# A second layer's seven products a unit: runs of four and three in place of pairs

## The chip, the cores and the metric

One Trainium2 chip, one of its cores. The metric is the device time of one execution in microseconds (us). TensorE does the matmuls and writes PSUM (eight banks), ScalarE and VectorE copy from PSUM and do the elementwise work, SyncE issues DMAs.

## The reference

Attention of a small state over `x` (8 batches, 8 heads, 512 positions and 32 state rows, width 64), and then two layers on its 4352 rows of 512 values:

```python
x = _attn_ref(x, state)                      # 8 x 544 rows of 512
h = np.maximum(x @ moe_w_in, 0.0)            # 512 -> 2048
x = (s * (h * h) + b) @ moe_w_out            # 2048 -> 512
h = np.maximum(x @ moe2_w_in, 0.0)           # the second layer
return (h * h) @ moe2_w_out
```

All in float32. The kernel splits each float32 operand into a high and a low part and adds three matmuls (high-high, high-low, low-high).

## The kernel before

The first 679 us hold the attention and the first layer; the change leaves them as they are. The second layer (`second_layer`, L716) goes through the rows in six parts: five of six tiles of 128 rows, and a last one of four. A part goes through eight units. A unit makes 256 columns of the hidden layer and multiplies them by the output weights.

The hidden columns of a unit are a 2 x 2 block product (two halves of the width 512, two halves of the part's rows, two blocks of 128 columns) with seven products in place of eight. The order is `PRODUCTS = (1, 6, 2, 5, 7, 3, 4)` (L54); this text calls them m0 to m6 by their place. Each product (L635) is six matmuls with 384 moving columns (256 in the last part). They lie in two PSUM banks of their own, pools `psa` and `psb`, taken in turns by the step's number. m0, m1, m3 and m4 begin a bank anew; m2, m5 and m6 add to what the bank still holds from m0, m3 and m4. So after each product, `drain` (L725) issues the instruction that reads the bank: ScalarE copies or rectifies m0, m2 and m3 (L654), VectorE adds m1 (`u2`, which also needs the copy of m0), m4 (`u3`, which also needs `u2`), m5 and m6 (L728). The next product on that bank waits for it. Behind the drains come the square and the split of the hidden values into `g` (L664, L668), partly one or two steps later.

The second product of a unit, hidden times output weights, is `mm2_second` (L672): for each of two blocks of 128 hidden columns and each tile of rows three matmuls with 512 moving columns (`o`, L686), 36 in a unit of six tiles, 24 in one of four. They add up in a bank per tile over the eight units of a part; behind the last ones the banks are copied out (L705, L707). `mm2_second(i - 1)` is issued during unit i, in shares: at each odd step, counted over all units, so much of it as corresponds to the place m. As a unit has seven steps, pairs of products and shares of about ten output matmuls alternate, and pairs lie across the border of two units. In unit 0 the share comes from the first layer's last 24 matmuls, of 256 columns.

Engines work in the order of issue. Behind each step's share, `jobs` issues what else is due there: in units 0 to 7 the sums and splits of the second input weights (L547, L555, L559) and the halves of the second output weights, 128 x 1024 each (L213 on ScalarE, L215 on VectorE), and in units 3, 4, 7 and 8 of the parts the inputs of the next part (`x_bias` L598, sums L607, `x_hi` L617 on ScalarE, `x_lo` L621 on VectorE). The last `x_lo`, for m6, is issued at m4 of the new part's first unit. From unit 8 on, `w_load` (L564) fetches a product's weights for two units later, behind the product.

Of the kernel before, what the change touches and what calls it, by code (L numbers as in the profile page):

```python
# [61 lines left out]
def attn_mlp2(ctx: ExitStack, tc: tile.TileContext, xT, xn, st, w_in1, w_out1, w_in2, w_out2, s_in, b_in, out):  # L62
# [34 lines left out]
    def pst(name, pool=None):  # L97
        return (pool or next(banks)).tile([P, 512], F32, tag="ps", name=name)
# [419 lines left out]
    def half(n):  # L518
        return len(parts[n]) // 2 * P
# [115 lines left out]
    def product(i, m, o, start):  # L635
        n, _ = units[i]
        w = w_at(i % 2, m).rearrange("p (h i c) -> p h i c", h=2, i=2)
        x = x_view(n, m)
        for k in range(2):
            for a, b in ((0, 0), (0, 1), (1, 0)):  # L640
                nc.tensor.matmul(  # L641
                    out=o, lhsT=w[:, a, k, :], rhs=x[:, b, k, :], start=(start and k + a + b == 0),
                    stop=(k + a == 2), skip_group_check=True,
                )
        w_load(i + 2, m)
# [26 lines left out]
    def mm2_second(i):  # L672

        n, u = units[i]
        nt = len(parts[n])
        if u == 0:
            for t in range(nt):
                pool, tag = (pa, "acc") if t < 4 else (psc, "ps")
                acc2[t] = pool.tile([P, 512], F32, tag=tag, name=f"o{n}{t}")
        for f in range(2):  # L680
            fa = 2 * u + f
            wh, wl = (w[:, fa % FQ, :] for w in W["o2", fa // FQ])
            for t in range(nt):
                g = g2[i, f][:, :, t * P : (t + 1) * P]
                for e, (l_, r_) in enumerate(((g[:, 0], wh), (g[:, 0], wl), (g[:, 1], wh))):
                    nc.tensor.matmul(  # L686
                        out=acc2[t], lhsT=l_, rhs=r_, start=(fa == 0 and e == 0), stop=(fa == NF - 1 and e == 2)
                    )
                    if fa == NF - 1 and e == 2:
                        out_tile(n, t)  # L690
                    yield
# [24 lines left out]
    def second_layer(between, rest):  # L716
# [84 lines left out]
        for i, (n, u) in enumerate(units):  # L801
            th = half(n)
            if i:
                flow.append((mm2_second(i - 1), 6 * len(parts[units[i - 1][0]])))
            for m, p in enumerate(PRODUCTS):
                step = i * len(PRODUCTS) + m
                pool = (psa, psb)[step % 2]
                if p in (1, 6, 5, 7):
                    c[p] = pst(f"m{p}", pool)[:, :th]
                out = c[{2: 1, 3: 5, 4: 7}.get(p, p)]  # L810
                product(i, m, out, p in (1, 6, 5, 7))
                drain(i, m, out)
                if step % 2:
                    while len(flow) > 1:
                        for _ in flow.pop(0)[0]:
                            pass
                        done = 0
                    upto = flow[0][1] * (m + 1) // len(PRODUCTS)
                    for _ in itertools.islice(flow[0][0], upto - done):
                        pass  # L820
                    done = upto
                for fn in jobs.pop((i, m), []):
                    fn()
# [208 lines left out]
    with tc.manual_schedule():  # L1032
# [50 lines left out]
        assert not side, sorted(side)  # L1083
        last = range(len(order) - LAG, len(order))
        second_layer(between, itertools.chain(*(mm2(*order[i], gs.pop(i)) for i in last)))


# [39 lines left out]
```

## Time and profile before

| | us |
|---|---|
| median of 3 runs | 1398.97 |
| lowest and highest | 1397.71, 1399.82 |
| the profiled execution | 1398.62 |
| its span, first to last instruction | 1396.8 |
| TensorE busy, share of the span | 1379.9, 99% |
| VectorE busy | 765.1, 55% |
| ScalarE busy | 759.2, 54% |

The mean granted clock of TensorE over the span is 0.991 of full speed. Matmuls are pipelined: one starts before the one ahead has ended, so a row's duration is longer than the distance to the next start, and a busy share of 99% does not mean that no time could be saved. Distances between starts are what the prediction works with.

### The profile page before, as it was taken

What the parts mean: (1) busy time and instruction counts of PE and PEld (TensorE: products, weight loads), DVE (VectorE), ACT (ScalarE), POOL (GpSimd) and SP (SyncE); (2) the same over time, 40 slices, a digit from 0 to 9 for tenths busy, and PEclk for the clock granted to TensorE, in tenths of its full rate; (3) what the DMA queues carried; (4) which work ended last, traced back from release to release, by engine and by line L of the source; (5) the groups of instructions that cost most, each with busy time, mean ns of one, the idle gap of its engine ahead of it and who ended that gap; (6) DMA issues with size and microseconds to landing.
All of it is one profiled execution on the core that took longest, in us unless ns stands there. A gap on an engine that the chain in (4) does not pass through costs nothing.

```text
span 1396.8 us, 20319 instructions
## 1 busy us (share of the span) xinstructions
PE 1379.9 (99%) x7822; PEld 1169.0 (84%) x7822; DVE 765.1 (55%) x1496; ACT 759.2 (54%) x1492; POOL 0.7 (0%) x7
## 2 busy tenths in 40 slices
PE   6999999999999999999999999999999999999998
PEld 4777777778777777889998999989999889998897
DVE  7888645555555867445677544453444435333433
ACT  5777656656666656557655543363344335433543
POOL 0000000000000000000000000000000000000000
PEclk7899999999999999999999999999999999999999
DMA  7365232332414241302673655445345533543652
GB/s 251 112 219 185 91 108 78 103 127 76 153 47 148 78 152 61 114 0 99 196 250 136 193 162 160 119 148 160 114 129 174 166 116 118 160 142 106 207 156 84
DMA packets 88432, 188.50 MB, mean 135 GB/s; under 512 B 8592, under 2 KB 25232, under 8 KB 85776
## 3 DMA queue, kind: packets, MB, share of 16 engines
q1 hardware_dynamic: 88192, 187.07, 42.2%
q8 instruction: 62, 1.02, 0.3%
q14 instruction: 34, 0.28, 0.1%
q10 hardware_dynamic: 144, 0.13, 0.0%
HBM read 144.18 MB, written 42.99 MB: 134 GB/s over the span
## 4 chain that ended last, share of the span: by engine, by line
PE 98%; DVE 1%; ACT 0%; issue 0%; POOLq 0%; POOL 0%
PE o L686 27%; PE acc L481 27%; PE m L641 24%; PE h L451 15%; PE S L263 2%; PE sr L416 1%; PE on L1030 1%; PE S L291 1%; PE sc L263 1%; PE tp L396 0%; DVE V L141 0%; DVE V L146 0%; PE S L306 0%; DVE m L365 0%; DVE t L366 0%; DVE t L379 0%
## 5 line engine op out<-in xcount | busy, mean ns | idle before, releaser
L481 PE MATMUL acc<-g,o1h 128*128 128x512 f32 (+1 forms) x1152 | 341.2, 379 | 0.0
L481 PEld LDWEIGHTS acc<-g,o1h 128*128 128x128 f32 x1152 | 211.4, 188 | 41.9 <-issue 2.2
L481 PE MATMUL acc<-g,o1l 128*128 128x512 f32 (+1 forms) x576 | 217.6, 378 | 0.4 <-DVE o1l L189 0.4
L451 PE MATMUL h<-aT,S 128*128 128x512 f32 x768 | 203.0, 400 | 3.0 <-ACT S L309 1.9
L451 PEld LDWEIGHTS h<-aT,S 128*128 128x128 f32 x768 | 142.6, 190 | 58.5 <-issue 10.9
L641 PE MATMUL m<-xw 128*128 128x384 f32 (+1 forms) x1008 | 183.1, 328 | 0.0
L641 PEld LDWEIGHTS m<-xw 128*128 128x128 f32 x1008 | 171.6, 188 | 7.5
L464 DVE TENSOR_TENSOR g<-r,g 128x512 fp32r<-128x512 f32 (+1 forms) x144 | 94.7, 658 | 112.0 <-ACT g L460 112.0
L654 ACT ACTIVATE sc<-sc 128x384 f32<-128x384 f32 (+1 forms) x144 | 72.8, 505 | 152.2 <-DVE sc L728 150.6
L458 ACT ACTIVATE r<-h 128x512 f32<-128x512 f32 (+1 forms) x144 | 82.1, 570 | 125.0 <-PE h L451 124.9
L654 ACT ACTIVATE v<-m 128x384 f32<-128x384 f32 (+1 forms) x96 | 45.5, 474 | 152.8 <-PE m L641 152.2
L481 PEld LDWEIGHTS acc<-g,o1l 128*128 128x128 f32 x576 | 108.4, 188 | 21.2 <-DVE o1l L189 0.9
L686 PE MATMUL o<-o2h,xw('g', 0)_6322 128*128 128x512 f32 x364 | 121.2, 392 | 0.0
L686 PE MATMUL o<-o2h,xw('g', 1)_6323 128*128 128x512 f32 x364 | 121.1, 392 | 0.0
L686 PE MATMUL o<-o2h,xw('g', 2)_6324 128*128 128x512 f32 x360 | 119.7, 392 | 0.0
L728 DVE TENSOR_TENSOR v<-m,r 128x384 f32<-128x384 f32 (+1 forms) x48 | 25.7, 535 | 167.3 <-PE m L641 167.3
L641 PE MATMUL m<-xw,xw('odd', 0)_6203 128*128 128x384 f32 (+1 forms) x576 | 107.3, 328 | 0.0
L641 PEld LDWEIGHTS m<-xw,xw('odd', 0)_6203 128*128 128x128 f32 x576 | 98.4, 188 | 3.8
L459 ACT ACTIVATE r<-r 128x512 f32<-128x512 f32 (+1 forms) x144 | 87.7, 609 | 4.6
L460 ACT ACTIVATE g<-r 128x512 fp32r<-128x512 f32 (+1 forms) x144 | 87.6, 609 | 4.6
L111 DVE TENSOR_TENSOR S<-S,S 128x512 fp32r<-128x512 f32 x54 | 34.8, 686 | 91.3 <-ACT S L110 91.3
L641 PE MATMUL m<-xw,xw('odd', 1)_6204 128*128 128x384 f32 (+1 forms) x432 | 79.3, 327 | 0.0
(150 smaller groups left out, 1909.4 us busy)
## 6 DMA issues: line engine op xcount, KB each, us to landing
xw<-w2s SPq DMA_DIRECT2D x140, 256.0 KB, 2.8
xw('odd', 0)_6203<-w2s SPq DMA_DIRECT2D x20, 1024.0 KB, 4.9
xw('odd', 1)_6204<-w2s SPq DMA_DIRECT2D x20, 768.0 KB, 4.3
i1r<-w_in SPq DMA_DIRECT2D x16, 512.0 KB, 5.2
xn<-xn SPq DMA_DIRECT2D x8, 1024.0 KB, 8.6
o1r<-w_out SPq DMA_DIRECT2D x16, 512.0 KB, 4.7
x<-ot SPq DMA_DIRECT2D x32, 256.0 KB, 2.9
i2r<-w_in SPq DMA_DIRECT2D x16, 512.0 KB, 5.2
```

The lines of the kernel that those rows point to most:

```text
L111: nc.vector.tensor_tensor(out=lo, in0=src, in1=hi.bitcast(F32), op=ALU.subtract)
L263: nc.tensor.matmul(out=outs[r][k * NS : (k + 1) * NS], lhsT=state[rows, r, k, :], rhs=moving(rows, k), start=True, stop=True, skip_group_c ...
L451: nc.tensor.matmul(out=hp, lhsT=l_, rhs=r_, start=(i == 0), stop=(i == len(ops) - 1))
L458: nc.scalar.activation(out=r, in_=hp, func=ACTF.Relu)
L459: nc.scalar.activation(out=r, in_=r, func=ACTF.Square)
L460: nc.scalar.activation(out=g[:, 0], in_=r, func=ACTF.Copy)
L464: nc.vector.tensor_tensor(out=g[:, 1], in0=r, in1=g[:, 0].bitcast(F32), op=ALU.subtract)
L481: nc.tensor.matmul(out=o, lhsT=l_, rhs=r_, start=(opens and i == 0), stop=(closes and i == 2))
L641: nc.tensor.matmul(out=o, lhsT=w[:, a, k, :], rhs=x[:, b, k, :], start=(start and k + a + b == 0), stop=(k + a == 2), skip_group_check=True,)
L654: nc.scalar.activation(out=c, in_=src, func=func)
L686: nc.tensor.matmul(out=acc2[t], lhsT=l_, rhs=r_, start=(fa == 0 and e == 0), stop=(fa == NF - 1 and e == 2))
L728: add = lambda o, x, y: nc.vector.tensor_tensor(out=o, in0=x, in1=y, op=ALU.add)
```

## The change

The share of output matmuls is issued behind m3 and behind m6 of each unit, in place of behind each odd step:

```diff
                 out = c[{2: 1, 3: 5, 4: 7}.get(p, p)]
                 product(i, m, out, p in (1, 6, 5, 7))
                 drain(i, m, out)
-                if step % 2:
+                if m in (3, 6):
                     while len(flow) > 1:
                         for _ in flow.pop(0)[0]:
                             pass
                         done = 0
                     upto = flow[0][1] * (m + 1) // len(PRODUCTS)
```

So m0 to m3 stand in one run, then 20 output matmuls (36 x 4 // 7; 13 with four tiles), then m4 to m6, then the other 16 (11). The banks go on in turns by the step's number: A, B, A, B, A, B, A in an even unit, the other way round in an odd one. Drains and jobs keep their steps.

## Rows read from the trace of the kernel before

**Rows 1.** The page's chain that ended last, by line.
```profile
PE o L686 27%; PE acc L481 27%; PE m L641 24%; PE h L451 15%; PE S L263 2%; PE sr L416 1%; PE on L1030 1%; PE S L291 1%; PE sc L263 1%; PE tp L396 0%; DVE V L141 0%; DVE V L146 0%; PE S L306 0%; DVE m L365 0%; DVE t L366 0%; DVE t L379 0%
```
**Rows 2.** Waits of TensorE: us in total, times, longest; last of seven.
```profile
PE acc L481 <- DVE o1l L189: 0.4, 1, 0.4
```
**Rows 3.** Timeline of TensorE, one pair: start, us, engine, line, tiles, count.
```profile
1009.28 1.23 PE L641 MATMUL m<-xw,xw('odd', 0)_6203 128*128 128x384 f32 x6
1010.35 1.20 PE L641 MATMUL m<-xw,xw('odd', 1)_6204 128*128 128x384 f32 x6
1011.39 0.39 PE L686 MATMUL o<-o2h,xw('g', 1)_6323 128*128 128x512 f32 x1
```
**Rows 4.** Timeline of TensorE, first layer, from one run of twelve to its end.
```profile
147.87 0.61 PE L481 MATMUL acc<-g,o1h 128*128 128x512 f32 x2
...
150.59 1.52 PE L451 MATMUL h<-aT,S 128*128 128x512 f32 x6
```
**Rows 5.** Timeline of TensorE, the first pair of units 22 and 24.
```profile
1018.33 2.27 PE L641 MATMUL m<-xw 128*128 128x384 f32 x12
...
1049.68 2.27 PE L641 MATMUL m<-xw 128*128 128x384 f32 x12
```
**Rows 6.** Timeline in the last part: products, output matmuls, two drains.
```profile
1327.09 1.60 PE L641 MATMUL m<-xw 128*128 128x256 f32 x12
1328.01 0.38 ACT L654 ACTIVATE sc<-m 128x256 f32<-128x256 f32 x1 [0.92 <-PE m L641]
1328.53 0.40 PE L686 MATMUL o<-o2h,xw('g', 1)_6323 128*128 128x512 f32 x1
...
1330.14 1.60 PE L641 MATMUL m<-xw 128*128 128x256 f32 x12
1331.05 0.42 DVE L728 TENSOR_TENSOR v<-m,r 128x256 f32<-128x256 f32 x1 [3.48 <-PE m L641]
```
**Rows 7.** Timeline of the drains, six tiles: copy of m3, `u3`, `u2`.
```profile
1010.54 0.49 ACT L654 ACTIVATE v<-m 128x384 f32<-128x384 f32 x1 [2.88 <-PE m L641]
...
1011.59 0.56 DVE L728 TENSOR_TENSOR v<-m,r 128x384 f32<-128x384 f32 x1 [2.96 <-PE m L641]
...
1020.71 0.56 DVE L728 TENSOR_TENSOR r<-m,v 128x384 f32<-128x384 f32 x1 [2.46 <-PE m L641]
```
**Rows 8.** Timeline of a wait in the first layer: VectorE, TensorE, weight load.
```profile
61.78 0.68 DVE L189 TENSOR_TENSOR o1l<-v,o1h 128x512 fp32r<-128x512 f32 x1
...
62.52 0.50 PE L481 MATMUL acc<-g,o1l 128*128 128x512 f32 x1 [0.42 <-DVE o1l L189]
62.86 0.62 PE L481 MATMUL acc<-g,o1h 128*128 128x512 f32 x2
...
62.52 0.19 PEld L481 LDWEIGHTS acc<-g,o1l 128*128 128x128 f32 x1 [0.85 <-DVE o1l L189]
```
**Rows 9.** Timeline of unit 8: m4 and m5, and the last `x_lo`.
```profile
807.73 2.27 PE L641 MATMUL m<-xw 128*128 128x384 f32 x12
...
809.94 0.55 DVE L621 TENSOR_TENSOR xw<-x,xw 128x384 fp32r<-128x384 f32 x1
```
**Rows 10.** Timeline of units 0 and 1: TensorE, ScalarE's and VectorE's splits, `u2`.
```profile
679.07 2.25 PE L641 MATMUL m<-xw 128*128 128x384 f32 x12
...
690.25 0.40 PE L686 MATMUL o<-o2h,xw('g', 0)_6322 128*128 128x512 f32 x1
...
681.84 0.55 DVE L728 TENSOR_TENSOR r<-m,v 128x384 f32<-128x384 f32 x1
...
689.56 1.05 ACT L213 ACTIVATE o2h<-o2f 128x1024 fp32r<-128x1024 f32 x1
...
690.87 1.21 DVE L215 TENSOR_TENSOR o2l<-o2f,o2h 128x1024 fp32r<-128x1024 f32 x1
...
693.13 0.55 DVE L728 TENSOR_TENSOR r<-m,v 128x384 f32<-128x384 f32 x1
```
**Rows 11.** Busy us (instructions) by engine, granted clock, DMA share, GB/s.
```profile
60.00:70.00 10.00, 9.58 (x68) 6.85 (x67) 8.84 (x16) 7.38 (x15) 0.00 (x0) 1.00 0.68 214
```

## The prediction

> **What bounds the kernel now.** I read the chain of waits first. TensorE holds 98% of it, and three lines hold most of that: the output products (`o`, L686), the first layer's (`acc`, L481) and the seven products of a unit (`m`, L641) [rows 1]. The waits of TensorE come next: the last of its seven is 0.4 us in the first layer, and none stands at L641 or L686 [rows 2]. So the second layer has no stall to remove. What is left is the distance from one matmul to the next, which the timeline shows, and whether the new order makes TensorE wait for the copies out of its two banks.
>
> **What the new order removes.** Alone on its kind, a 384-column matmul follows the one before after 0.1733 us: the second product of a pair takes 1.04 us for six [rows 3]. A 512-column one follows after 0.2267 us: twelve in the first layer take 2.72 us [rows 4]. Two units of a part with six tiles hold 84 of the first and 72 of the second, 14.56 + 16.32 = 30.88 us. They take 31.35 us, from the first matmul of one even unit to that of the next [rows 5]. The 0.47 us over falls to the changes of kind. The first product of a pair takes 1.07 us where the second takes 1.04 [rows 3], so part of it lies just behind the change; the rest lies in the output matmuls behind a product. Two units make seven changes there and back, 0.067 us each. The new order makes four in two units, so it saves 3 x 0.067 = 0.20 us in two units, 0.10 in one. Of the 40 units with six tiles, unit 0 has its products beside the first layer's last 24 matmuls of 256 columns, and I count nothing there: 39 x 0.10 = 3.9 us. In the last part (four tiles, products of 256 columns) twelve products take 1.44 us, 0.12 each, and seven output matmuls 1.61 us where 7 x 0.2267 = 1.59 [rows 6]: 0.02 a change, 12 changes fewer over eight units, 0.3 us. Together **4.2 us** less. Both ends: nothing, if the excess is a debt of each matmul and not of the change, and 4.2 if it is all of the change. I take 4.2, since the second product of each pair already runs without it.
>
> No instruction is added or taken away: the same matmuls, copies and DMAs are issued, each engine but TensorE keeps its order except for the twelve or so copies that end a part, and the weight loads of SyncE still follow their product, two units ahead of use. I cost these at nothing.
>
> **What the new order adds: a third product on a bank just left.** In a pair, each bank had the output matmuls between two uses. In a run the products lie on banks A, B, A, B, then A, B, A. So m2 waits for ScalarE's copy of m0, m3 for VectorE's sum of m1 (`u2`), m6 for VectorE's sum of m4 (`u3`). I time each from the start of the last matmul of the drained product. The copy starts after 0.37 us on either engine (ScalarE at 1010.54, where the product's last matmul started 0.17 before the next product at 1010.35); `u2`, which waits for two engines, after 0.45 us (1020.71 against 1018.33 + 1.07 + 5 x 0.1733 = 1020.27); they last 0.49 and 0.56 us [rows 3, 5, 7]. From the end of such an instruction to the released matmul go 0.05 us, and its weight load starts with it, not ahead: the next matmul then follows after 0.34 us where 0.227 is usual, so 0.11 us of weight load lie bare [rows 8]. The waiting product's own turn comes after 7 x 0.1733 = 1.21 us.
>
> - Six tiles: m2 could go at 0.37 + 0.49 + 0.05 + 0.11 = 1.02, m3 at 0.45 + 0.56 + 0.16 = 1.17, m6 at 0.37 + 0.56 + 0.16 = 1.09. All are before 1.21: no stall where the draining engine is free.
> - Last part: the turn comes after 7 x 0.12 = 0.84 us. Drains start after 0.32 us and last 0.38 on ScalarE and 0.42 on VectorE [rows 6]. m2 goes at 0.32 + 0.38 + 0.16 = 0.86, 0.02 late; m3, with the 0.07 more of `u2`, at 0.97, 0.13 late in all; m6 at 0.90, 0.06 late. That is 0.2 us a unit, eight units: **1.6 us**.
> - The first unit of each later part: m6 also needs the last piece of the new inputs (`x_lo` of its second half), which VectorE has behind `u3`. In unit 8 it ended at 810.49, and the last matmul of m4 started at 807.73 + 0.89 = 808.62 [rows 9]: 1.87 + 0.16 = 2.03 us, while m6's fifth matmul is due at 11 x 0.1733 = 1.91. Ten output matmuls cover this now. 0.12 us four times and, in the same way, 0.2 once with 256 columns: **0.7 us**.
> - Units 0 and 1: VectorE and ScalarE carry the splitting of the second output weights there. In unit 0 `u2` began at 681.84 behind such a piece; + 0.55 + 0.16 is 682.55, and m3, now without six matmuls before it, is due at 679.07 + 3 x 1.045 = 682.20: 0.35 late [rows 10]. In unit 1 the first layer's last copies and a split of 1.05 us stand before ScalarE's copy of m0. Its first product would start at 690.25 (where 24 first-layer matmuls and eight products were done) - 1.04 + 0.35 = 689.56. The last copy then ends near 690.2, the split near 691.2, the copy of m0 near 691.6, so m2 goes at 691.8, 0.1 late. VectorE's half of the split follows ScalarE's at 691.2, and from its start to `u2` it was 693.13 - 690.87 = 2.26 us: `u2` at 693.5, m3 at 694.2, due at 692.8: 1.4 late. Together **1.85 us**, between 0.5 (if VectorE drains as in a free unit) and 4 (if units 2 and 3 repeat it; I leave them out since 16 output matmuls, 3.6 us, now lie before each first product).
>
> The sum is -4.2 + 1.6 + 0.7 + 1.85 = -0.05 us. From the profiled execution's 1398.62 us (span 1396.8 and 1.8 around it) this gives 1398.6. The median of the runs lies 0.35 above, so I forecast **1399.0 us**, and 1397.4 to 1400.8 for this case alone.
>
> Two rules are weighed here. The weight load that waited along with its matmul stood idle 0.85 us until the same VectorE instruction ended [rows 8]. The Trainium skill ("TensorE: Matmul & The Clock Gate", section "What happens when you issue a matmul") says that TensorE pulls weight loads ahead of matmuls in flight. By that nothing would lie bare behind a wait, and the last part would lose 0.2 us instead of 1.6; the row speaks against it. The same page of the Trainium skill (section "A second HAM failure mode: psum-queue depth-cycling") says that short idle times of TensorE while it cycles through banks make its clock fall and rise again. Here TensorE stood still for 0.42 us at 62.1, and the granted clock of 60 to 70 us was 1.00 [rows 8, 11].
>
> **The rivals.**
> - *The waits cost little (faster).* The weight load goes ahead of its wait, and VectorE has room in unit 1. Then m3 of the last part is 0.865 - 0.84 = 0.03 late (0.2 in all), m6 of a new part starts in time, and units 0 and 1 lose 0.24 and 0.4: -4.2 + 0.9 = -3.3, 1395.7 us. For it: TensorE has no wait at all in the second layer now. Against it: the bare weight load in the row. 0.18.
> - *A weight load behind a wait costs its full length (slower).* The row gives it 0.19 us, not 0.11 [rows 8]. The point at which it decides is m3 in every unit with six tiles: 0.45 + 0.56 + 0.05 + 0.19 = 1.25 against 1.21, 0.035 x 39 = 1.3 us. In the last part m3 is 0.215 late in all and m6 0.145: 0.36 x 8 = 2.9. New parts 1.1, the beginning 2.1: 7.4 - 4.2 = +3.2, 1402.2 us. Against it: after the wait the next matmul came 0.34 us later, not 0.42. 0.10.
> - *Fewer changes save nothing.* The excess of 0.47 us in two units belongs to the number of matmuls and moves behind the longer runs. Then only the waits are left: 1399.0 + 4.2 = 1403.2 us. Against it: the second product is free of it. 0.07.
> - *The clock falls* from 2.4 to 1.2 GHz for a while in the last part, where the waits come every few microseconds. A stretch of 10 us of matmuls would take up to 10 us more. Against it: the row of 60 to 70 us. 0.01. It is the rule of the Trainium skill's page "TensorE: Matmul & The Clock Gate" on cycling through banks.
>
> **How the numbers follow.** The forecast has 0.64. A measurement of this kernel tells about 0.2% from no change, 2.8 us: faster is below 1396.2, slower above 1401.8. The forecast's own range lies inside; faster 0.18, slower 0.10 + 0.07 + 0.01 = 0.18. The range for 8 in 10 takes in the first two rivals, 1395.6 to 1402.4, and leaves out the last two and the tails.
>
> **What would show each step.** Right: two units of the middle parts take 31.15 us; the runs of four and three show 24 and 18 matmuls with the excess only in the first product; the waits of TensorE list L641, with the longest, over 1 us, near 694 us, and small ones behind the drains after 1300 us; none at m2, m3 or m6 of the middle units, but one at m6 in the first unit of each part. Wrong: two units still take 31.3 us or more, or waits stand in each middle unit at m3, or the last part takes as long as before.

## The result, and the profile after

The changed kernel takes **1416.24 us** (median of 4 runs, 1414.89 to 1418.80), the kernel before 1399.31 beside it (4 runs): a ratio of 1.0122 [1.0107, 1.0138]. The prediction said 1399.0, no change. It is slower by 17 us, outside the range. The profiled execution of after is the run of 1418.80 us. In it the second layer, from unit 0's first matmul to the end, takes 735.6 us where it took 717.75 before: +17.9. The first layer, which the change leaves alone, ends 2.2 us later than in the profile of before. That end lies between 678.0 and 681.3 us in the profiles of this study, so distances within the second layer are compared.

The page of after: busy time by engine, then its chain of work by engine and by line.

```profile
PE 1382.3 (98%) x7822; PEld 1170.5 (83%) x7822; DVE 766.4 (54%) x1496; ACT 752.6 (53%) x1492; POOL 0.7 (0%) x7
...
PE 92%; DVE 3%; DMA 2%; SPq 1%; ACT 1%; issue 0%; ACTq 0%; DVEq 0%
PE acc L481 26%; PE o L686 25%; PE m L641 22%; PE h L451 14%; PE S L263 2%; PE sr L416 1%; DMA out<-ot 1%; DMA o1r<-w_out 1%; PE tp L396 1%; SPq L331 0%; PE S L291 0%; PE sc L263 0%; ACT sc L654 0%; DVE ot L707 0%; ACT ot L705 0%
```

Against [rows 1] the two lines of the second layer, L686 and L641, lost four points, and among the new names are `DMA out<-ot`, the store of finished rows, and L705 and L707, the copies into the buffers of that store. A chain that passes through the output's stores in mid-kernel is the first sign. The waits of TensorE (total, times, longest), as in [rows 2]:

```profile
PE m L641 <- ACT v L654: 12.1, 6, 3.7
...
PE m L641 <- DVE r L728: 0.9, 1, 0.9
```

Six products wait for ScalarE's copy of m0 (`v`, L654), 12.1 us in all. The waits of the other engines say why that copy is late:

```profile
ACT ot L705 <- DMA out<-ot: 16.9, 5, 5.2
...
DVE ot L707 <- DMA out<-ot: 8.8, 5, 2.6
```

There are five borders between parts in the second layer, and five times each engine waits for a store. The copies of a part's rows stand in the share behind m6 of the next part's first unit, so the waits show in the unit behind it (9, 17, 25, 33, 41). The longest is in unit 25. The timeline of after there, all engines but most weight loads and sums left out: TensorE runs m0 and m1, then nothing until 1082.95.

```profile
1075.11 0.57 ACT L705 COPY ot<-o 128x512 f32<-128x512 f32 x1
...
1076.09 0.59 ACT L705 COPY ot<-o 128x512 f32<-128x512 f32 x1 [0.41 <-PE o L686]
...
1076.18 1.28 DVE L707 COPY ot<-o 128x512 f32<-128x512 f32 x2
...
1076.89 3.65 SPq L714 DMA_DIRECT2D out<-ot  x8
...
1077.25 2.27 PE L641 MATMUL m<-xw,xw('odd', 0)_6203 128*128 128x384 f32 x12
1080.07 0.69 DVE L707 COPY ot<-o 128x512 f32<-128x512 f32 x1 [2.60 <-DMA out<-ot]
1080.63 2.23 SPq L710 DMA_DIRECT2D out<-ot  x4
1081.92 0.58 ACT L705 COPY ot<-o 128x512 f32<-128x512 f32 x1 [5.24 <-DMA out<-ot]
1082.40 0.50 ACT L654 ACTIVATE v<-m 128x384 f32<-128x384 f32 x1
...
1082.93 0.56 DVE L728 TENSOR_TENSOR r<-m,v 128x384 f32<-128x384 f32 x1 [2.18 <-ACT v L654]
1082.95 2.63 PEld L641 LDWEIGHTS m<-xw,xw('odd', 0)_6203 128*128 128x128 f32 x12 [3.75 <-ACT v L654]
1082.95 3.14 PE L641 MATMUL m<-xw,xw('odd', 0)_6203 128*128 128x384 f32 x12 [3.43 <-ACT v L654]
```

The pool `op` has four buffers, the part six tiles. The first four copies (two on each engine) fill them. The fifth, on VectorE, and the sixth, on ScalarE, wait until a store has landed and freed a buffer. In this part two tiles are stored in four pieces each (L714), and SyncE takes 3.65 us to issue these eight. Behind the sixth copy, in ScalarE's queue, stands the copy of m0: it runs at 1082.40, 4.28 us after m0's last matmul began (1077.25 + 5 x 0.1733), where a free ScalarE takes 0.37. m2, which goes on in m0's bank, waits for it.

The same order at the border between the first two parts, ScalarE in after, and the place that answers to it in before:

```profile
822.29 0.57 ACT L705 COPY ot<-o 128x512 f32<-128x512 f32 x1
823.24 0.59 ACT L705 COPY ot<-o 128x512 f32<-128x512 f32 x1 [0.39 <-PE o L686]
826.81 0.58 ACT L705 COPY ot<-o 128x512 f32<-128x512 f32 x1 [2.98 <-DMA out<-ot]
827.29 0.50 ACT L654 ACTIVATE v<-m 128x384 f32<-128x384 f32 x1
```

```profile
812.54 1.06 ACT L705 COPY ot<-o 128x512 f32<-128x512 f32 x2
814.45 0.49 ACT L654 ACTIVATE v<-m 128x384 f32<-128x384 f32 x1 [0.85 <-PE m L641]
...
816.79 0.57 ACT L705 COPY ot<-o 128x512 f32<-128x512 f32 x1
```

Before, the share of the odd step 63 (unit 9, m0) was issued behind m0's drain, and the last copy came behind it, at 816.79, when its buffer was free. Now the share at m6 of unit 8 carries all six copies, in front of that drain. The order of the stores seems to add to the wait, though no run here changes it: SyncE issues them in the order of the tiles, and the first tile is VectorE's, whose copy began at 823.36. So the first store was issued at 824.07, while ScalarE's first copy had ended at 822.86.

In unit 1 the first layer's last copies (L504, L506) do the same through the same pool. TensorE, then ScalarE of after:

```profile
691.80 2.25 PE L641 MATMUL m<-xw,xw('odd', 0)_6203 128*128 128x384 f32 x12
697.72 1.58 PE L641 MATMUL m<-xw,xw('odd', 0)_6203 128*128 128x384 f32 x6 [3.66 <-ACT v L654]
700.19 2.29 PE L641 MATMUL m<-xw,xw('odd', 0)_6203 128*128 128x384 f32 x6 [0.89 <-DVE r L728]
702.28 0.63 PE L686 MATMUL o<-o2h,xw('g', 0)_6322 128*128 128x512 f32 x1
702.71 0.63 PE L686 MATMUL o<-o2l,xw('g', 0)_6322 128*128 128x512 f32 x1
```

```profile
691.79 0.46 ACT L504 ACTIVATE ot<-acc,s_sb 128x256 f32<-128x256 f32 x1
695.87 0.47 ACT L504 ACTIVATE ot<-acc,s_sb 128x256 f32<-128x256 f32 x1 [3.62 <-DMA x<-ot]
696.24 1.05 ACT L213 ACTIVATE o2h<-o2f 128x1024 fp32r<-128x1024 f32 x1
697.18 0.48 ACT L654 ACTIVATE v<-m 128x384 f32<-128x384 f32 x1
```

The output matmuls at 702 follow each other after 0.43 us, not 0.227: the clock has fallen. The windows of after, busy time (instructions) of PE, PEld, DVE, ACT, POOL, then the granted clock, the DMA share and GB/s:

```profile
698.00:706.00 8.00, 7.11 (x22) 5.83 (x22) 5.61 (x12) 6.77 (x15) 0.00 (x0) 0.57 1.00 342
706.00:714.00 8.00, 8.00 (x40) 7.08 (x39) 4.40 (x9) 2.48 (x5) 0.00 (x0) 1.00 0.31 115
824.00:828.00 4.00, 2.83 (x16) 2.44 (x15) 1.51 (x4) 1.19 (x3) 0.00 (x0) 1.00 0.75 288
1077.00:1083.00 6.00, 2.57 (x15) 2.18 (x13) 1.22 (x3) 1.08 (x3) 0.00 (x0) 1.00 0.58 187
1083.00:1088.00 5.00, 5.00 (x18) 4.59 (x19) 1.51 (x3) 3.58 (x8) 0.00 (x0) 0.66 0.44 121
```

Behind the waits of 3.66 us (unit 1) and 3.43 us (unit 25) TensorE ran at 1.2 GHz, half of the full clock, for a few microseconds (0.57 and 0.66 of it granted on the mean of these stretches). At the wait of 1.17 us in unit 9 (824 to 828) it kept 1.00.

Where the 17.9 us lie, by the distance from m0 of a unit to m0 of the next:

| unit | before | after | the excess |
|---|---|---|---|
| two middle units | 31.35 | 31.16 to 31.19 | -0.2 |
| units 0 and 1 | 25.80 | 10.50 + 23.35 | 8.05 |
| 9, 17, 25, 33 | 15.68 (half of two) | 17.01, 17.35, 20.88, 17.03 | 9.95 over 15.58 |
| 41 (256 columns) | 10.55 (half of two) | 11.97 | 1.27 over 10.70 |
| others of the last part | 10.55 | 10.70 | 0.15 each |

The excess of units 0 and 1 and of the five borders is 19.3 us. Units 2 to 39 save 0.087 each (28 middle units take 15.673 on the mean before and 15.586 after), 3.3 in all. With 0.15 in eight units of the last part (1.2), 0.12 in four first units (0.5) and 0.2 more in unit 40, the first unit of the last part, it makes the 17.9.

### The profile page after: what moved, and what is told of

It reads as the page before. It is cut to its first block, busy times and chain, and to the rows that moved or that the text cites. A ratio compares the mean times of both kernels' runs of the same rounds, so it can differ in the third digit from the quotient of the medians.

```text
span 1416.9 us, 20318 instructions
## 1 busy us (share of the span) xinstructions
PE 1382.3 (98%) x7822; PEld 1170.5 (83%) x7822; DVE 766.4 (54%) x1496; ACT 752.6 (53%) x1492; POOL 0.7 (0%) x7
## 3 DMA queue, kind: packets, MB, share of 16 engines
q8 instruction: 62, 1.02, 0.3%
## 4 chain that ended last, share of the span: by engine, by line
PE 92%; DVE 3%; DMA 2%; SPq 1%; ACT 1%; issue 0%; ACTq 0%; DVEq 0%
PE acc L481 26%; PE o L686 25%; PE m L641 22%; PE h L451 14%; PE S L263 2%; PE sr L416 1%; DMA out<-ot 1%; DMA o1r<-w_out 1%; PE tp L396 1%; SPq L331 0%; PE S L291 0%; PE sc L263 0%; ACT sc L654 0%; DVE ot L707 0%; ACT ot L705 0%
## 5 line engine op out<-in xcount | busy, mean ns | idle before, releaser
L654 ACT ACTIVATE sc<-sc 128x384 f32<-128x384 f32 (+1 forms) x144 | 72.7, 505 | 248.5 <-DVE sc L728 247.0
L641 PE MATMUL m<-xw 128*128 128x384 f32 (+1 forms) x1008 | 176.4, 328 | 0.1
L641 PEld LDWEIGHTS m<-xw 128*128 128x128 f32 x1008 | 169.2, 188 | 5.1 <-DVE xw L621 0.7
L686 PE MATMUL o<-o2h,xw('g', 0)_6322 128*128 128x512 f32 x364 | 119.7, 396 | 0.0
L686 PE MATMUL o<-o2h,xw('g', 1)_6323 128*128 128x512 f32 x364 | 117.9, 391 | 0.0
L686 PE MATMUL o<-o2h,xw('g', 2)_6324 128*128 128x512 f32 x360 | 116.6, 390 | 0.0
L641 PE MATMUL m<-xw,xw('odd', 0)_6203 128*128 128x384 f32 (+1 forms) x576 | 103.6, 333 | 12.9 <-ACT v L654 12.1
L654 ACT ACTIVATE v<-m 128x384 f32<-128x384 f32 (+1 forms) x96 | 45.3, 472 | 128.3 <-PE m L641 127.1
L641 PEld LDWEIGHTS m<-xw,xw('odd', 0)_6203 128*128 128x128 f32 x576 | 97.9, 191 | 17.2 <-ACT v L654 13.9
L728 DVE TENSOR_TENSOR r<-m,v 128x384 f32<-128x384 f32 (+1 forms) x48 | 25.7, 535 | 112.7 <-PE m L641 91.5
```

Source lines behind the costliest of these rows:

```text
L641: nc.tensor.matmul(out=o, lhsT=w[:, a, k, :], rhs=x[:, b, k, :], start=(start and k + a + b == 0), stop=(k + a == 2), skip_group_check=True,)
L654: nc.scalar.activation(out=c, in_=src, func=func)
L686: nc.tensor.matmul(out=acc2[t], lhsT=l_, rhs=r_, start=(fa == 0 and e == 0), stop=(fa == NF - 1 and e == 2))
L728: add = lambda o, x, y: nc.vector.tensor_tensor(out=o, in0=x, in1=y, op=ALU.add)
```

## The experiments

Ten kernels, in the order of three questions: is it the buffers, what is left without them, and what the turns are worth alone. The kernel before had a median of 1398.2 to 1398.8 us beside them, and ratios are to that. Theory A is the wait for an output buffer in front of m0's drain. Rival B says that the six copies in front of that drain are the cause whatever their buffers, rival C that the stores crowd the DMA queue.

**e1_out.** The fifth and sixth output tile of a part take a buffer of another pool, so that no copy waits for a store. The first layer's copies stay.

```diff
 def out_tile(n, t):
-    ot = op.tile([P, 512], F32, tag="o", name="ot")
+    pool, tag = (op, "o") if t < 4 else (gp, "g")
+    ot = pool.tile([P, 512], F32, tag=tag, name="ot")
```

> The changed kernel, with the output copies of tiles 5 and 6 of a part in a buffer of another pool (gp, idle by then) in place of the pool of four. Theory A (the fifth and sixth copy wait until the store of an earlier one has landed, and ScalarE's copy of m0 stands behind them, so m2 waits): the waits in units 9, 17, 25, 33 and 41 go, 11.2 us of them by the unit times 17.01, 17.35, 20.88, 17.03, 11.97 against 15.58 (10.7 in the last part); those of unit 1 stay: 1405 us. Rival B (m0's copy is late because six copies stand ahead of it on the two engines, whatever their buffers): 1416. Rival C (the stores crowd the DMA queue and everything behind it): 1416.

1405.38 us, 1.0051 [1.0034, 1.0067]. Units 9 and 25 take 15.59 and 15.58, unit 41 10.68; unit 1 stays at 23.12. TensorE and ScalarE in unit 25, with the same instructions as above: no copy waits for a store, and four products run without a gap.

```profile
1070.92 0.59 ACT L706 COPY ot<-o 128x512 f32<-128x512 f32 x1 [0.77 <-PE o L686]
1071.98 0.49 ACT L654 ACTIVATE v<-m 128x384 f32<-128x384 f32 x1 [0.48 <-PE m L641]
```

```profile
1070.72 4.35 PE L641 MATMUL m<-xw,xw('odd', 0)_6203 128*128 128x384 f32 x24
```

Theory A holds for the five borders, 1416.24 - 1405.38 = 10.9 of the 17 us. The six copies and the stores are still where they were, so B and C, which foresaw 1416, fall.

**e2_both.** The same for the first layer's last copies.

```diff
+    pool, tag = (op, "o") if j < B or t < 2 else (gp, "g")   # in evac, L501
```

> As the kernel before it in this list, and the first layer's last two copies (its tiles 3 and 4, in unit 0) in the other pool too. Theory A: the 3.7 us wait of unit 1 goes as well, with the clock's fall behind it; units 0 and 1 then lose the 1.85 us of the prediction against 8 us now: 1399 us. Rivals B and C: as the changed kernel, 1416.

1399.29 us, 1.0004 [0.9995, 1.0013]. Unit 1 takes 17.25. So the other 6 us are the same wait, and with it gone the time is the forecast's. What is left in unit 1 is the wait of m3 that the prediction priced at 1.4 us:

```profile
688.66 3.50 PE L642 MATMUL m<-xw,xw('odd', 0)_6203 128*128 128x384 f32 x18
693.37 1.31 PE L642 MATMUL m<-xw,xw('odd', 0)_6203 128*128 128x384 f32 x6 [1.21 <-DVE r L730]
```

**e3_order.** The other half of the same cause: four buffers as they were, but the copies of the last two tiles (of each part, shown here, and in the same way of the first layer) are kept back and issued behind the drain of the next unit's m1.

```diff
-                        out_tile(n, t)
+                        late.append(lambda t=t: out_tile(n, t)) if t > 3 else out_tile(n, t)
...
+                while m == 1 and late:
+                    late.pop(0)()
```

> The changed kernel, with the copies of the last two tiles (of the first layer and of each part) issued behind the drain of the next unit's m1, buffers as they were: they may wait for the stores, but not ahead of m0 and m1. Theory A: 1399 to 1402 (they can still hold up the copy of m2, which has 4.6 us). Rival B: the same. Rival C: 1410 or more. Together with the two kernels before it this tells buffer from order.

1399.09 us, 1.0002 [0.9993, 1.0012]. ScalarE, then TensorE in unit 25:

```profile
1067.64 0.49 ACT L658 ACTIVATE v<-m 128x384 f32<-128x384 f32 x1 [1.84 <-PE m L645]
...
1071.10 0.59 ACT L709 COPY ot<-o 128x512 f32<-128x512 f32 x1 [1.02 <-DMA out<-ot]
```

```profile
1066.38 4.38 PE L645 MATMUL m<-xw,xw('odd', 0)_6203 128*128 128x384 f32 x24
```

The copy still waits 1.02 us for a store, and it costs TensorE nothing: what stands behind it is the copy of m2, whose bank is wanted again only behind the share of output matmuls. So neither the wait nor the order alone makes the loss: it takes a waiting copy in front of a drain that TensorE soon needs.

**e10_sixth.** Only the sixth tile takes the other pool (`t < 5` in place of `t < 4` in e1_out; the first layer's copies stay).

> The changed kernel, with the sixth tile's copy alone (ScalarE's) in the other pool; the fifth (VectorE's) still waits for the first store. Theory A with ScalarE's queue as the place: m0's copy is free, u2 behind the fifth copy is late in unit 25 alone (1080.76 + 0.47 + 0.56 + 0.16 against 1080.40, 1.0 us): 1405.4 + 1.0 = 1406.4. If the fifth copy's wait is as bad as the sixth's: 1412 or more.

1406.89 us, 1.0058 [1.0045, 1.0072]. The sixth copy, ScalarE's, is worth 1416.2 - 1406.9 = 9.3 us; the fifth, VectorE's, 1406.9 - 1405.4 = 1.5; the first layer's 1405.4 - 1399.3 = 6.1. Of the 1.5 the units show 1.0, all but 0.1 of it in unit 25 (16.57 against 15.58). There, with only the fifth waiting, VectorE's sum of m1 comes late, and m3 waits 0.70 us:

```profile
1076.11 0.69 DVE L708 COPY ot<-o 128x512 f32<-128x512 f32 x1 [2.60 <-DMA out<-ot]
1076.72 0.55 DVE L729 TENSOR_TENSOR r<-m,v 128x384 f32<-128x384 f32 x1
```

**e7_before_bufs.** The control: the kernel before with the two buffer edits of e2_both.

> Control: the kernel before, pairs and all, with nothing but the two buffer edits of e2_both. Theory A: its copies never waited for a store, so it gains nothing: 1398.6 and no change of the unit times. If the buffers are a gain of their own, below 1397.

1398.95 us, 1.0004 [0.9994, 1.0013], its units unchanged. The buffers are no gain of their own; they only take away what the new order made late.

**e4_seams.** The changed kernel with its four buffers, but the old turns (odd steps) in the first two units of each part (`NF // 2` is 8); at the borders the copies then lie as before.

```diff
-                if m in (3, 6):
+                if step % 2 if i % (NF // 2) < 2 else m in (3, 6):
```

> The changed kernel, with the old pairs in the first two units of each part (12 of 48 units), where copies and stores of the part before and the inputs of the new part fall; runs of four and three in the other 36. Theory A, and the prediction's turns: 30 units of six tiles save 0.10 us each, the six of the last part lose 0.15 each, nothing else: 1399.3 - 3.0 + 0.9 = 1397.2. If the runs cost something in every unit: above 1399.3.

1398.53 us, 0.9997 [0.9988, 1.0006]. The 17 us are gone by order alone, a second time. Most of the miss of 1.3 us lies at the border from pairs to runs: unit 2 took 16.54 where a middle unit with runs takes 15.59, with one wait of 0.7 us on VectorE's `u2`, which I had counted as free.

**e5_trim.** e2_both, pairs in units 0 to 2 and in the last part, runs between, and the last input pieces (`x_hi`, `x_lo`) one step earlier.

```diff
-                job(7, 11 * e // count, lambda m=m, i=i: x_hi(n, m, i))
+                job(7, 10 * e // count, lambda m=m, i=i: x_hi(n, m, i))
...
-                if m in (3, 6):
+                if m in (3, 6) if 3 <= i < 40 else step % 2:
```

> Both sets of copies in the other pool, as in e2_both; the old pairs in units 0 to 2 and in the last part, runs of four and three in units 3 to 39; and the inputs of a new part split one step earlier (the last x_lo at m3 of its first unit, not at m4). If the turns are worth 0.067 us each and no wait is left: 37 units x 0.10 = 3.7 us less than before, 1398.6 - 3.7 = 1394.9. If the runs save nothing in sum (the excess belongs to the matmuls): 1398.6.

1396.81 us, 0.9989 [0.9980, 0.9998]. The first units of the parts take 15.58, without excess, so the wait for `x_lo` is gone as expected. Unit 3 took 17.91, 0.9 more than before (17.04): again a wait of 0.7 us on `u2` in the first unit with runs, where VectorE still splits weights. The time is 1.9 above the expectation; unit 3 is 0.9 of it, and 36 units that save 0.085 in place of 0.10 are 0.5. The rest stays open.

**e9_trim4.** e5_trim with runs from unit 4 on (`4 <= i < 40`).

> e5_trim with its runs of four and three from unit 4 on in place of unit 3, so that no share is left over at the border: the wait of 0.7 us on VectorE's u2 in unit 3 goes. 36 units x 1.5 turns x 0.067 = 3.6 us less than before: 1394.8.

1396.00 us, 0.9979 [0.9970, 0.9988]. No wait is left in the second layer. It misses its expectation by 1.2 us. Its second layer takes 714.79 us, 2.96 less than before, so the 36 units save 0.08 each in place of 0.10: that is 0.6 of the miss. Another 0.4 is the kernel before, 1398.83 beside it where the expectation began from 1398.4.

**e6_seven.** e5_trim with one run of seven products, the share behind m6 alone, and the second block's `g` split at m3 and m4. At the border into unit 3 the last six output matmuls of unit 1 come behind m6 of unit 3, when the split of unit 3's first block has overwritten the buffer with the hidden values that they should read (the buffers of `g` are three, in turns).

> As e5_trim, with one run of seven and one share of 36 in units 3 to 39 (the split of the second block's hidden values two to three steps later, so that ScalarE's queue is free for the drains). One turn a unit in place of two, if the turn is the price: 37 x 0.067 = 2.5 us less than e5_trim, 1392.4, units of 15.51 us. If the third products on a bank now wait (m4 for the copy of m2), the same as e5_trim or slower.

1401.74 us, 1.0022 [1.0013, 1.0031]. So this kernel adds up wrong values there, the six waited 4.0 us for ScalarE's split, and unit 3 took 24.55 us. That is my slip at the border, and the time of this kernel tells nothing of runs of seven; its middle units do: 15.52 on the mean, against 15.59 with two turns and 15.67 with 3.5.

**e8_seven4.** Runs of seven in units 4 to 39, where no share is left over at the border; pairs elsewhere; buffers and pieces as in e9_trim4.

```diff
-                if m in (3, 6):
+                if m == 6 if 4 <= i < 40 else step % 2:
...
+                later = (3, 4) if 3 <= i < 39 else (0, 1)
-                after[i + 1, 0] = [lambda: g_hi(i, 1, 1, q)]
+                after[i + 1, later[0]] = [lambda: g_hi(i, 1, 1, q)]
```

> One run of seven and one share of 36 in units 4 to 39, pairs in units 0 to 3 (which end with no share left over, so no wait of 4 us on the hidden values in unit 3) and in the last part; buffers and the early input split as in e5_trim. If each turn there and back costs 0.067 us: 36 units x 2.5 turns x 0.067 = 6.0 us less than before, less 0.3 in unit 39: 1398.4 - 5.7 = 1392.7, units of 15.51 us. If the runs only move the excess: 1398.

**1393.30 us, 0.9960 [0.9947, 0.9974]**: faster than both kernels, and 0.6 from its expectation. A unit of it, 42 products in one run:

```profile
1016.93 7.47 PE L642 MATMUL m<-xw 128*128 128x384 f32 x42
1024.24 0.39 PE L687 MATMUL o<-o2h,xw('g', 0)_6322 128*128 128x512 f32 x1
```

From one kind to the other 7.31 us go by, 42 x 0.1733 = 7.28: the excess over the steady distance is 0.03 here and the rest in the first output matmuls behind.

## Why the prediction was wrong

**The step that failed** is the second paragraph of "What the new order removes": "each engine but TensorE keeps its order except for the twelve or so copies that end a part ... I cost these at nothing." The prediction saw that these copies move, and did not ask what they wait for and what stands behind them. At each border six copies take their buffers from a pool of four, and the fifth and sixth put a wait for a store in front of the drains of m1 and m0. e1_out prices that at 10.9 us for the five borders.

**Unit 1 failed by the same step.** The terms "the last copy then ends near 690.2" and "m2 goes at 691.8, 0.1 late" took the first layer's copies as free too. Here the prediction saw the queue in front of m0's copy, and missed only that two of the four copies wait for a store. In after the first of the stores was issued at 693.36, the two copies began at 695.32 and 695.87, the last ended at 696.3 (the prediction's 690.2 is 692.4 here, since the layer begins 2.2 us later), and m2 was 3.66 us late. e2_both prices it at 6.1 us, the fallen clock among it.

**The other terms held**, as far as rows and e2_both can tell:
- Turns: two middle units take 31.16 to 31.19, predicted 31.15. The term was a little too large: a unit saves 0.08 to 0.09 us and not 0.10, 3.2 in all over units 2 to 39, predicted 3.9. e6 and e8 give about the same price from the other side: 1.5 turns fewer saved 0.08 a unit, one more 0.07.
- Last part: 10.70 a unit against 10.55, 8 x 0.15 = 1.2 us net, predicted 1.6 - 0.3. In the timeline of after m0 to m3 take 3.00 us where 24 x 0.12 = 2.88 is their own:

```profile
1364.86 3.16 PE L641 MATMUL m<-xw 128*128 128x256 f32 x24
1367.86 0.40 PE L686 MATMUL o<-o2h,xw('g', 2)_6324 128*128 128x512 f32 x1
```

- The first units of later parts: 15.68 to 15.73 against 15.58, predicted 0.12 more.
- m3 of unit 1, once the copies are out of the way: 1.21 us, predicted 1.4; units 0 and 1 together 1.97 us longer than before, predicted 1.85.
- Middle units: no wait at m2, m3 or m6, as foreseen.

With the failed step taken away the time is 1399.3 (e2_both) or 1399.1 (e3_order), where the sum said 1399.0. That it agrees so closely is in part luck: the second layer of e2_both takes 718.43 us, 0.68 more than before, where the sum said 0.05 less, and the kernel before had 1398.63 beside it where the sum began from 1398.97.

**The rivals.** A weight load that goes ahead of its wait would leave a unit of the last part where it was (0.03 - 0.04 us), one that costs its full length would add 0.36 - 0.04; both fall to the 0.15. In after the weight load and the matmul behind the longest waits start together (1082.95), as in [rows 8]. "Fewer changes save nothing" falls to the middle units. The clock's fall, given 0.01 for the last part, did not come there, but came in units 1 and 25, as a follower of the long waits: unit 25's twelve matmuls behind the wait took 2.94 us where 2.08 is usual and the next five 1.99 where 1.15 is, and in unit 1 m3 and eight output matmuls took 5.38 where 2.88 is usual: 1.7 + 2.5 = 4.2 of the 17 us. The Trainium skill ("TensorE: Matmul & The Clock Gate", section "A second HAM failure mode: psum-queue depth-cycling") puts such a fall to short idle times between groups of matmuls; here the four waits of 1.14 to 1.47 us left the clock at 1.00, and those of 3.43 and 3.66 us were followed by 1.2 GHz.

## What to carry to other kernels

When a step moves in the order of issue, look at every instruction that moves with it on the other engines: what buffer it takes, how many the pool has, and whose landing frees one; then what is queued behind it. A copy that waits for a store costs nothing until a drain that is soon needed stands behind it; then the wait, less what the drain has to spare, goes to TensorE (3.43 of 5.24 us in unit 25), here twice with a slower clock after it. Either another buffer or a later place in the queue takes it away.

## What was not expected of the hardware

- The issue of a store took SyncE about as long for a quarter of a tile, 64 KB (L714), as for a whole one, 256 KB (L710): about 0.4 us (least, median and most in ns, unit 25). So a tile in four pieces takes 1.8 us (3.65 for the eight pieces of two tiles), and the part whose rows are stored in pieces had the longest wait, 5.24 us where unit 9 had 2.98.

```profile
L714 SPq DMA_DIRECT2D out<-ot x8: 350/424/433, 1076.9 to 1080.1; - x8
L710 SPq DMA_DIRECT2D out<-ot x4: 332/385/408, 1080.6 to 1082.5; - x4
```

- A turn from 384 to 512 columns and back costs 0.05 to 0.07 us: 1.5 turns fewer in a unit saved 0.08, one more fewer 0.07. It lies partly in the first matmuls of either kind: in after's middle unit the run of 24 takes 4.19 us, 0.03 over 24 x 0.1733, and the run of 20 takes 4.57, 0.04 over 20 x 0.2267.

```profile
1030.36 4.35 PE L641 MATMUL m<-xw 128*128 128x384 f32 x24
1034.55 0.39 PE L686 MATMUL o<-o2h,xw('g', 0)_6322 128*128 128x512 f32 x1
...
1039.12 3.31 PE L641 MATMUL m<-xw 128*128 128x384 f32 x18
```
